# Packed attention and a feed-forward layer on one core: a new order table, aligned buffers at the end of SBUF, another ending of the last rows

## Chip, core and metric

The kernel runs on one core of one Trainium2 chip. The metric is the device time of the whole program in microseconds, as a median of runs. Engines are named as in the profile: PE (TensorE, with its weight loads as PEld), DVE (VectorE), ACT (ScalarE), POOL (GpSimd), SP (SyncE, which here only issues transfers).

## The reference

Eight batches of eight heads with 576 tokens of width 64 go through an attention over 32 learned packs: first the packs look at the tokens, then the tokens look at the packs. The result, 4608 tokens of width 512, goes through a feed-forward layer of width 2048.

```python
def sm_attn(qq, kk, vv):
    s = scale * np.matmul(qq, kk.transpose(0, 1, 3, 2))
    s = s - np.max(s, axis=-1, keepdims=True)
    a = np.exp(s)
    a = a / (np.sum(a, axis=-1, keepdims=True) + 1e-09)
    return np.matmul(a, vv)
p_packed = sm_attn(p, k, v)
attn = sm_attn(q, p_packed, p_packed)      # 8 x 8 x 576 x 64
x = attn.transpose(0, 2, 1, 3).reshape(4608, 512)
h = x @ w_in                               # 512 x 2048, float64
g = h * (1.0 / (1.0 + np.exp(-h)))
out = (g @ w_out).astype(np.float32)       # 2048 x 512, float64
```

## The kernel before

**Precision.** A float32 product is made from two parts of each factor, a rounded upper part and the rest (names end in hi and lo), and three products of those: hi·hi, hi·lo, lo·hi.

**Weights.** w_in and w_out arrive as the bits of float64 numbers and are turned into float32 on the chip, in 20 chunks. Each chunk n goes through the steps fetch (a transfer on SP's queue, L238), scale (two instructions on ACT, L244 and L245), clip (DVE, L249), sign (DVE, L253), shift (DVE, L261), join (POOL or DVE, L265); a chunk of w_out also through upper (ACT, L273) and lower (DVE, L277). Chunks 0 to 7 have 128 x 512 numbers, the others 128 x 1024.

**Attention of a batch.** For the packs: scores (L284), their largest values, exps on ACT (L331), a turn and a spread by 16 small transfers (L363), the packed product (L384), its scaling by the shares (L394, which writes the tile pp), and a turn back into ppT (L403, L407). For the tokens, in two halves: scores (L284), transposes on DVE (L420), largest values (L468), exps (L488), sums, shares, a turn, and the split into a_hi (L518, ACT) and a_lo (L522, DVE). Packed rows are multiplied by w_in ahead of time (L532, split at L550 and L553), so a batch's hidden values come from a product of its shares with pw_hi and pw_lo (L587).

**Feed-forward.** The work is cut into 144 units. A unit has a first product (L587), silu on ACT, the split of its values into g_hi and g_lo, and a product by w_out (L643) that adds into the four banks acc. Units 0 to 31 belong to batches 0 and 1 and run while the weights are still converted; they make g_hi on ACT (L599) and g_lo on DVE (L605). From unit 36 on, the units of batches 2 to 7 take two blocks of w_out at once in seven products in place of eight, for which some sums of values are made on POOL (L619 to L621), g_hi on ACT (L633) and g_lo on DVE (L637), and some sums of weights are kept in DRAM (sums_of_w). Those sums are formed once for each pair p of blocks, by DVE (L721), POOL (L726 to L729), ACT (L734) and DVE (L738). The 16 units of a batch are two passes of eight, one for each half of the tokens; each pass ends in pair_rows, which reads the four banks and stores 256 rows, and the next pass begins in the same banks. 32 rows of each half are left over; four of the units (32 to 35, 68 to 71, 104 to 107, 140 to 143) hold those of two batches each, and end in rest_rows (L767). The last of them ends the program.

**What sets the order.** Nothing here is found by a scheduler except for POOL's queue and the waits. A table of tokens, ORDER (lines 54 to 123), lists every step: a letter or two for the step, a number for the batch, unit or chunk. The instructions of PE, DVE, ACT and SP are issued in the order of that table. wf5 is the fetch of chunk 5, ws, wc, wz, wi, wj, wu and wl the further steps of a chunk; a small a with a letter is a step of attention (as scores of the packs, ax exps of the packs, aa packed product, aS, aT, aM the scores, transposes and largest values of the tokens); pf, pp, pu, pl belong to the packs' product by w_in; h, g, l, o are first product, silu with g_hi, g_lo and product by w_out of an early unit, and B, G, N, I, F, L, O the steps of a later one (B the first, O the last product); r, R, ru, rl, rk make the sums of weights of a pair; k, v and q load a batch; Wn runs n small matmuls; E is pair_rows, Y rest_rows.

**Buffers.** Pools named with side "right" are laid out from the far end of SBUF. First comes win there (the weights of w_in, int32), whose space goes to the pair buffers later: w_pair, w_sums, and the sums that come back from DRAM. The tile pp lies in the pool tmp on the other side.

## Time and profile before

| | us |
|---|---|
| median of three runs | 695.2 |
| lowest and highest run | 695.13, 695.38 |
| the profiled execution | 696.58 |
| its span | 694.80 |

The rows come from the profiled execution. A window is given in microseconds from the start of its span. The mean granted clock of TensorE over the span was 0.993 of full speed. An engine's busy time is the time in which an instruction of it ran; its idle time in brackets is put down to what came last.

### The profile page before, as it was taken

To read this page: it belongs to the slowest core of one execution; us is meant where nothing else is said; L and a number is where in the kernel's file an instruction comes from. 1 tells how busy PE (TensorE), PEld (TensorE's weight loads), DVE (VectorE), ACT (ScalarE), POOL (GpSimd) and SP (SyncE) were. 2 spreads that over 40 slices of the span, in tenths; PEclk is the share of its full clock that TensorE was granted. 3 is DMA by queue.
4 is the path that set the end of the run, shared out by engine and by line. 5 is a ranking of instruction groups with operands and counts; after the bars stand their busy time and mean duration, and the time that the engine had idled before them with its cause. 6 is when DMAs were issued, how large, how long until landed. Compare 5 with 4: busy or idle time off the path is not lost.

```text
span 694.8 us, 14721 instructions
## 1 busy us (share of the span) xinstructions
PE 674.6 (97%) x5958; PEld 593.1 (85%) x5958; DVE 425.9 (61%) x588; ACT 386.5 (56%) x641; POOL 232.4 (33%) x336
## 2 busy tenths in 40 slices
PE   7699999999999999999999999999999999999996
PEld 5477776788878998999888998899888998899995
DVE  5988989896774536753666525853665435663433
ACT  5787887453645535563555634755554753564431
POOL 0102054343203432544423333353241353435420
PEclk9899999999999999999999999999999999999999
DMA  9747864675967768867797578874984738685531
GB/s 362 321 138 300 289 218 174 232 267 193 367 242 290 267 223 328 360 253 260 284 339 284 186 276 328 336 268 130 364 346 174 290 120 324 252 317 184 218 132 45
DMA packets 55107, 178.62 MB, mean 257 GB/s; under 512 B 21760, under 2 KB 25856, under 8 KB 47360
## 3 DMA queue, kind: packets, MB, share of 16 engines
q1 hardware_dynamic: 54944, 177.56, 69.0%
q8 instruction: 47, 0.77, 0.4%
q10 hardware_dynamic: 96, 0.13, 0.1%
q14 instruction: 20, 0.16, 0.1%
HBM read 149.42 MB, written 24.12 MB: 250 GB/s over the span
## 4 chain that ended last, share of the span: by engine, by line
PE 77%; DVE 10%; ACT 4%; DMA 4%; SPq 2%; issue 2%; POOL 1%; ACTq 0%; DVEq 0%
PE ps_acc L643 46%; PE ps_two L587 24%; PE ps_two L284 5%; DMA win<-in_w_out 2%; PE ps_two L384 2%; DMA sums_of_w<-sums_of_w 2%; SPq L363 2%; DVE tm L420 1%; DVE g_lo L605 1%; DVE w_raw L249 1%; DVE w_raw L253 1%; DVE g_lo L637 1%; DVE wo_lo L277 1%; DVE o L785 1%; DVE win L261 0%
## 5 line engine op out<-in xcount | busy, mean ns | idle before, releaser
L637 DVE TENSOR_TENSOR g_lo<-g,g_hi 128x896 fp32r<-128x896 f32 x96 | 106.4, 1116 | 131.2 <-ACT g_hi L633 128.4
L643 PE MATMUL ps_acc<-wo_hi,g_hi 128*128 128x256 f32 (+1 forms) x576 | 185.1, 321 | 0.8 <-DVE o L785 0.8
L643 PE MATMUL ps_acc<-wo_hi,g_lo 128*128 128x256 f32 (+1 forms) x576 | 183.9, 319 | 2.0 <-DVE g_lo L605 2.0
L643 PE MATMUL ps_acc<-wo_lo,g_hi 128*128 128x256 f32 (+1 forms) x576 | 183.6, 319 | 0.0
L587 PE MATMUL ps_two<-a_hi,pw_hi 128*128 128x288 f32 x512 | 153.1, 299 | 1.5 <-DVE tm L420 1.5
L619 POOL TENSOR_TENSOR g<-g 128x128 f32<-128x128 f32 x96 | 56.4, 587 | 290.7 <-ACT g L609 290.6
L587 PE MATMUL ps_two<-a_lo,pw_hi 128*128 128x288 f32 x512 | 151.4, 296 | 0.0
L587 PE MATMUL ps_two<-a_hi,pw_lo 128*128 128x288 f32 x512 | 151.4, 296 | 0.0
L633 ACT CAST g_hi<-g 128x896 fp32r<-128x896 f32 x96 | 89.8, 940 | 76.7 <-POOL g L621 45.0
L643 PEld LDWEIGHTS ps_acc<-wo_hi,g_hi 128*128 128x128 f32 x576 | 108.4, 188 | 16.3 <-issue 5.6
L643 PEld LDWEIGHTS ps_acc<-wo_hi,g_lo 128*128 128x128 f32 x576 | 108.7, 189 | 12.4 <-DVE g_lo L605 4.3
L643 PE MATMUL ps_acc<-sums_of_w,g_hi 128*128 128x256 f32 x576 | 116.7, 284 | 0.3 <-DMA sums_of_w<-sums_of_w 0.3
L643 PEld LDWEIGHTS ps_acc<-wo_lo,g_hi 128*128 128x128 f32 x576 | 108.5, 188 | 7.1 <-DVE wo_lo L277 0.3
L587 PEld LDWEIGHTS ps_two<-a_hi,pw_hi 128*128 128x128 f32 x512 | 96.7, 189 | 14.4 <-PE ps_two L284 6.7
L587 PEld LDWEIGHTS ps_two<-a_lo,pw_hi 128*128 128x128 f32 x512 | 96.6, 189 | 0.8
L643 PEld LDWEIGHTS ps_acc<-sums_of_w,g_hi 128*128 128x128 f32 x576 | 89.1, 189 | 9.3 <-issue 7.8
L587 PEld LDWEIGHTS ps_two<-a_hi,pw_lo 128*128 128x128 f32 x512 | 96.6, 189 | 0.0
L643 PE MATMUL ps_acc<-sums_of_w,g_lo 128*128 128x256 f32 x288 | 81.2, 282 | 0.0
L620 POOL TENSOR_TENSOR g<-g 128x256 f32<-128x256 f32 x96 | 75.0, 783 | 6.6
L609 ACT ACTIVATE g<-ps_two 128x512 f32<-128x512 f32 x96 | 56.9, 597 | 33.4 <-DVE g_lo L637 16.9
L643 PEld LDWEIGHTS ps_acc<-sums_of_w,g_lo 128*128 128x128 f32 x288 | 54.6, 190 | 0.3 <-DVE g_lo L637 0.3
L621 POOL TENSOR_TENSOR g<-g 128x128 f32<-128x128 f32 x96 | 52.3, 546 | 6.6
(129 smaller groups left out, 798.9 us busy)
## 6 DMA issues: line engine op xcount, KB each, us to landing
sums_of_w<-sums_of_w SPq DMA_DIRECT2D x96, 768.0 KB, 6.3
w_quarter<-w_in SPq DMA_DIRECT2D x22, 1024.0 KB, 6.9
kvq_t<-in_v SPq DMA_DIRECT2D x8, 1280.0 KB, 8.8
kvq_t<-in_pkT SPq DMA_DIRECT2D x7, 1216.0 KB, 10.4
out<-o SPq DMA_DIRECT2D x16, 512.0 KB, 3.2
kvq_t<-in_qT SPq DMA_DIRECT2D x7, 1152.0 KB, 8.1
w_raw<-in_w_in SPq DMA_DIRECT2D x6, 1024.0 KB, 6.1
sums_of_w<-w_sums SPq DMA_DIRECT2D x8, 768.0 KB, 3.8
```

What stands on the lines that cost most here:

```text
L249: nc.vector.tensor_scalar(up.bitcast(F32), up.bitcast(F32), TOP, -TOP, op0=ALU.min, op1=ALU.max)
L284: nc.tensor.matmul(bank(par)[NP * i : NP * i + NP], lhs(r, i), rhs(r, i), start=True, stop=True)
L363: nc.sync.dma_start(self.e1T[NP * at : NP * at + NP, : some.shape[1], i], some)
L384: nc.tensor.matmul(self.ps[NP * i : NP * i + NP, par * D : par * D + D], e, vs[:n, c, h * D : h * D + D], start=(c == 0), stop=(c == 4),)
L587: nc.tensor.matmul(bank, p[:, par, cols], a[:, par], start=(n == 0), stop=(n == len(todo) - 1))
L609: nc.scalar.activation(g[:, : 4 * P].rearrange("p (e s) -> p e s", e=2), made["h", u, None][..., :MAIN], AF.Silu)
L619: nc.gpsimd.tensor_tensor(x[:, 4], x[:, 0], x[:, 2], ALU.subtract)
L620: nc.gpsimd.tensor_tensor(x[:, 5:7], x[:, 0:5:4], one, ALU.subtract)
L621: nc.gpsimd.tensor_tensor(x[:, 7], x[:, 3], x[:, 6], ALU.add)
L633: nc.scalar.copy(both[0], g)
L637: nc.vector.tensor_tensor(g_lo, g, g_hi.bitcast(F32), ALU.subtract)
L643: nc.tensor.matmul(out, g[:, rows], w, start=(first and n == 0), stop=(last and n == 2), skip_group_check=True)
```

## The change

Three things are edited: the order table, the place of some buffers, and the last rows. The instructions stay the same in number and kind, except that ACT loads function tables 46 times in place of 42 and that the last rows' store is one transfer in place of four.

**The table.** All of ORDER is replaced; the diff shows one line of each version, from the place where unit 59's product and unit 60's follow one another.

**Buffers.** A new pool, edge, is the first on the right side. It holds pp in 504 float32 numbers for each partition, 2016 bytes, of which 128 numbers are used. All other buffers of the right side move down by that much; they stood at 224 bytes beyond a multiple of 256 and now stand at multiples of 256.

**The last rows.** In the last four products of a rest unit, the blocks n = 0 and 2, which add into bank 0, come ahead of n = 1 and 3, which add into bank 2. In rest_rows the two additions change places: first the one between two parts of what ACT copied out of bank 0, then the one that reads bank 2. The four stores of 32 rows, on SP's queue and for the last batches also on ACT's, become one of 128 rows on SP's.

```diff
 ORDER = """
...
-O58 I59 F59 L59 G60 I60 F60 L60 O59 N61 G61 ar4 aa4 pf19 an4 S61 B62 E3.0 S62 S63 I61 ai4 aj4 O60 N62 F61 G62 L61
...
+B61 F59 N61 ai4 S59 S61 O58 S60 pf19 S62 L59 G61 I60 F60 B62 O59 N62 L60 E3.0 G62 O60 I61 F61 aj4 aS4.0 L61 I62 pp19
...
 """
 
 TP_BUFS = 4
+EDGE = 504
 ON_TOKENS = (0,)
...
     at_right = [ExitStack(), ExitStack()]
+    edge = ent(tc.tile_pool(name="edge", bufs=1, side="right"))
...
         def scaled1(self):
-            self.pp = tmp.tile([P, P], F32, name="pp", bufs=1)
+            self.pp = edge.tile([P, EDGE], F32, name="pp")[:, :P]
...
     def rest_products(u):
         b, f, _ = units[u]
         first, last = f == 0, f + FJ == NF
-        for n in range(FJ):
+        for n in sorted(range(FJ), key=lambda n: n % 2) if last else range(FJ):
...
         if opened.get(("rest", b, 0)):
             nc.scalar.copy(o[:, 1], acc[0])
+            nc.vector.tensor_tensor(o[:, 1, high], o[:, 1, high], o[:, 1, low], ALU.add)
             nc.vector.tensor_tensor(o[:, 0], acc[2], o[:, 1], ALU.add)
-            nc.vector.tensor_tensor(o[:, 0, high], o[:, 0, high], o[:, 1, low], ALU.add)
         else:
             nc.scalar.copy(o[:, 0, low], acc[2][:, low])
             nc.vector.tensor_copy(o[:, 0, high], acc[2][:, high])
-        for n, (e, h) in enumerate((e, h) for e in range(2) for h in range(2)):
-            at = (b + e) * S + h * HS + MAIN
-            rows = slice((2 * e + h) * REST, (2 * e + h) * REST + REST)
-            (nc.scalar if n % 2 and b == B - 2 else nc.sync).dma_start(out[at : at + REST], o[rows, 0])
+        to = out[b * S : (b + 2) * S].rearrange("(n s) e -> n s e", s=HS)[:, MAIN:]
+        nc.sync.dma_start(to, o[:, 0])
```

What the new table moves is seen best in the instructions of one engine. In the changed kernel a line's number is one or two higher than in the kernel before.

The first place is the start of SP's queue, which issues the loads. L238 (later L240) fetches a chunk of weights, L197 (L199) loads packs and keys of batch 0, L216 (L218) its values, L206 (L208) its tokens. Before:

```order
L238 DMA w_raw<-in_w_in 128x512
L197 DMA kvq_t<-in_pkT 128x1280
L197 DMA kvq_t<-in_pkT 128x1152
L238 DMA w_raw<-in_w_out 128x512
L216 DMA kvq_t<-in_v 128x2560
L238 DMA w_raw<-in_w_in 128x512
L206 DMA rest<-in_qT 128x1280
L206 DMA o<-in_qT 128x1024
L238 DMA win<-in_w_out 128x512
L238 DMA w_raw<-in_w_out 128x512
```

After:

```order
L240 DMA w_raw<-in_w_in 128x512
L240 DMA w_raw<-in_w_out 128x512
L199 DMA kvq_t<-in_pkT 128x1280
L199 DMA kvq_t<-in_pkT 128x1152
L240 DMA w_raw<-in_w_in 128x512
L240 DMA w_raw<-in_w_out 128x512
L240 DMA win<-in_w_out 128x512
L218 DMA kvq_t<-in_v 128x2560
L208 DMA rest<-in_qT 128x1280
L208 DMA o<-in_qT 128x1024
```

The second chunk moves ahead of the keys, and three chunks that stood behind the values and the tokens now stand ahead of the values.

The second place is DVE around the g_lo of unit 21. In the stretch before it is the first g_lo row (the second is unit 22's); w_raw is chunk 19 at L249, L253 and L261 (L251, L255 and L263), and the rows on w_pair are the pair sums of p = 4. Before, from the step behind the g_lo of unit 20:

```order
L407 COPY ppT<-ps_two 128x128
L738 TENSOR_TENSOR w_sums<-w_pair,w_sums 128x1024
L277 TENSOR_TENSOR wo_lo<-w_raw,wo_hi 128x1024
L605 TENSOR_TENSOR g_lo<-g,g_hi 128x512
L721 TENSOR_TENSOR w_pair<-wo_hi,wo_lo 128x2x256
L721 TENSOR_TENSOR w_pair<-wo_hi,wo_lo 128x512
L249 TENSOR_SCALAR w_raw<-w_raw 128x1024
L253 SCALAR_TENSOR_TENSOR w_raw<-w_raw 128x1024
L261 TENSOR_SCALAR w_raw<-w_raw 128x1024
L553 TENSOR_TENSOR pw_lo<-ps_two,pw_hi 128x1024
```

After, from the lower part of chunk 18 on; the first g_lo row is unit 20's, and unit 21's and 22's are the last row:

```order
L279 TENSOR_TENSOR wo_lo<-w_raw,wo_hi 128x1024
L607 TENSOR_TENSOR g_lo<-g,g_hi 128x512
L251 TENSOR_SCALAR w_raw<-w_raw 128x1024
L255 SCALAR_TENSOR_TENSOR w_raw<-w_raw 128x1024
L422 STREAM_TRANSPOSE tm<-ps_two 128x288 x2
L263 TENSOR_SCALAR w_raw<-w_raw 128x1024
L422 STREAM_TRANSPOSE tm<-ps_two 128x288 x2
L723 TENSOR_TENSOR w_pair<-wo_hi,wo_lo 128x2x256
L723 TENSOR_TENSOR w_pair<-wo_hi,wo_lo 128x512
L470 TENSOR_REDUCE mx_1673<-tm 128x18
L607 TENSOR_TENSOR g_lo<-g,g_hi 128x512 x2
```

Clip, sign and shift of chunk 19, the pair sums, two pairs of transposes and a maximum of batch 2 have moved from behind the g_lo of unit 21 to ahead of it.

The third place is ACT at the exps of batch 2's packs (tm and den), among the silu values g of the early units around number 10. Before:

```order
L598 ACTIVATE g<-ps_two 128x512
L599 ACTIVATE g_hi<-ps_two 128x512
L600 ACTIVATE rest<-ps_two 128x64
L550 CAST pw_hi<-ps_two 128x1024
L331 ACT_TABLE_LOAD
L331 ACTIVATE tm,den<-tm,nm 128x576 x2
L598 ACT_TABLE_LOAD
L598 ACTIVATE g<-ps_two 128x512
L599 ACTIVATE g_hi<-ps_two 128x512
L600 ACTIVATE rest<-ps_two 128x64
L734 CAST w_sums<-w_pair 128x1024
```

After:

```order
L600 ACTIVATE g<-ps_two 128x512
L601 ACTIVATE g_hi<-ps_two 128x512
L602 ACTIVATE rest<-ps_two 128x64
L333 ACT_TABLE_LOAD
L333 ACTIVATE tm,den<-tm,nm 128x576
L600 ACT_TABLE_LOAD
L600 ACTIVATE g<-ps_two 128x512
L601 ACTIVATE g_hi<-ps_two 128x512
L602 ACTIVATE rest<-ps_two 128x64
L333 ACT_TABLE_LOAD
L333 ACTIVATE tm,den<-tm,nm 128x576
L600 ACT_TABLE_LOAD
```

The two exps, which stood behind one table load, are now parted by the silu of a unit, so that four loads stand there in place of two.

## Rows read from the trace of the kernel before

**Rows 1.** The page: busy time, share and instructions of each engine, and the busy tenths of DVE in 40 slices of 17.4 us each.

```profile
PE 674.6 (97%) x5958; PEld 593.1 (85%) x5958; DVE 425.9 (61%) x588; ACT 386.5 (56%) x641; POOL 232.4 (33%) x336
...
DVE  5988989896774536753666525853665435663433
```

**Rows 2.** The table by stage, for the stretch in which weights are still converted and the one from there to unit 143. Columns: window, its length, then busy time and instructions of PE, of its weight loads, of DVE, ACT and POOL, granted clock, DMA share, GB/s.

```profile
26.60:125.70 99.10, 95.46 (x726) 74.57 (x727) 92.04 (x128) 77.25 (x128) 27.20 (x19) 0.97 0.60 215
125.70:675.70 550.00, 547.09 (x4911) 493.72 (x4910) 309.96 (x413) 290.04 (x479) 203.44 (x310) 1.00 0.72 266
```

**Rows 3.** The chain of waits between 120 and 156 us, in order of time: start, length, what ran. L605 makes the g_lo of an early unit, L643 is a product by w_out.

```profile
126.05 0.69 DVE g_lo L605
...
126.79 2.79 PE ps_acc L643 x10
...
151.87 3.00 PE ps_acc L643 x12
```

**Rows 4.** The transfers of all queues between 8 and 13 us, and the first instructions of the packed product of batch 0 in PE's timeline (start, length, engine, line, what; in brackets the idle time before and its releaser).

```profile
DMA packets 355, 2.09 MB, mean 418 GB/s; under 512 B 37, under 2 KB 37, under 8 KB 238
...
12.23 1.73 PE L384 MATMUL ps_acc<-kvq_t,tm 128*32 128x64 f32 x80 [0.46 <-DVE tm L370]
```

**Rows 5.** Groups of instructions of ACT from 0 to 31 us, by line and shape: busy time, mean ns of one, idle time before and its releaser; these are the scale steps of one chunk. Below them DVE's first instruction on a weight in its timeline.

```profile
L244 ACT ACTIVATE w_raw<-w_raw 128x512 int32<-128x512 uint32 x4 | 2.7, 687 | 2.6 <-DMA w_raw<-in_w_in 2.6
L244 ACT ACTIVATE win<-win 128x512 int32<-128x512 uint32 x4 | 2.6, 660 | 0.9 <-DMA win<-in_w_out 0.9
L245 ACT ACTIVATE w_raw<-w_raw 128x512 f32<-128x512 f32 x4 | 2.6, 659 | 0.0
...
5.80 0.43 DVE L249 TENSOR_SCALAR w_raw<-w_raw 128x512 f32<-128x512 f32 x1 [5.80 <-ACT w_raw L245]
```

**Rows 6.** The table by stage, columns as in rows 2: to the end of the second g_lo of unit 0, from that of unit 4 to that of unit 16, and from there to that of unit 21.

```profile
0.00:39.00 39.00, 29.91 (x345) 22.35 (x345) 28.78 (x59) 25.45 (x48) 4.19 (x9) 0.91 0.85 338
63.03:126.74 63.71, 61.37 (x398) 48.31 (x397) 60.07 (x75) 49.24 (x73) 21.43 (x15) 1.00 0.59 205
126.74:147.82 21.08, 21.03 (x193) 17.01 (x194) 16.94 (x22) 12.87 (x22) 5.17 (x5) 1.00 0.73 267
```

**Rows 7.** DVE's timeline: the clip of chunk 13, clip and sign of chunk 17, then the pair sums of p = 4, clip and sign of chunk 19, and two transposes of batch 2.

```profile
86.57 0.69 DVE L249 TENSOR_SCALAR w_raw<-w_raw 128x1024 f32<-128x1024 f32 x1
...
111.38 2.38 DVE L249 TENSOR_SCALAR w_raw<-w_raw 128x1024 f32<-128x1024 f32 x1
113.80 1.23 DVE L253 SCALAR_TENSOR_TENSOR w_raw<-w_raw 128x1024 int32<-128x1024 int32 x1
...
147.74 1.28 DVE L721 TENSOR_TENSOR w_pair<-wo_hi,wo_lo 128x512 f32<-128x512 f32 x2
149.29 1.17 DVE L249 TENSOR_SCALAR w_raw<-w_raw 128x1024 f32<-128x1024 f32 x1 [0.27 <-ACT w_raw L245]
150.50 1.63 DVE L253 SCALAR_TENSOR_TENSOR w_raw<-w_raw 128x1024 int32<-128x1024 int32 x1
...
154.33 0.83 DVE L420 STREAM_TRANSPOSE tm<-ps_two 128x288 f32<-128x288 f32 x2
```

**Rows 8.** POOL's timeline around 151 us: the third of the four pair sums of p = 4.

```profile
151.13 1.60 POOL L728 TENSOR_TENSOR w_pair<-w_pair 128x256 f32<-128x256 f32 x1
```

**Rows 9.** Waits of PE from 199.5 to 675.7 us, by the line that waited and what released it: us in total, times, longest.

```profile
PE ps_two L587 <- DVE tm L420: 1.2, 5, 0.2
PE ps_two L284 <- DVE tm L420: 0.5, 2, 0.2
```

**Rows 10.** PE's timeline: two matmuls of unit 99, and the first of unit 140.

```profile
507.98 0.28 PE L643 MATMUL ps_acc<-sums_of_w,g_hi 128*128 128x256 f32 x1
508.31 0.39 PE L643 MATMUL ps_acc<-sums_of_w,g_lo 128*128 128x256 f32 x1
...
679.12 0.47 PE L643 MATMUL ps_acc<-wo_hi,g_hi 128*128 128x512 f32 x1 [0.75 <-DVE o L785]
```

**Rows 11.** The end of the program: ACT, DVE and the queues in the timeline, then the transfers from 690 us on and, for its size, one of 512 KB between 676 and 685 us (queue, number, KB each, median us from issue to landing).

```profile
689.66 0.59 ACT L769 COPY o<-ps_acc 128x512 f32<-128x512 f32 x1 [4.36 <-PE ps_acc L643]
...
690.40 0.69 DVE L770 TENSOR_TENSOR o<-ps_acc,o 128x512 f32<-128x512 f32 x1 [4.38 <-PE ps_acc L643]
691.12 0.42 DVE L771 TENSOR_TENSOR o<-o 128x256 f32<-128x256 f32 x1
691.57 0.80 SPq L778 DMA_DIRECT2D out<-o  x2
...
out<-o SPq DMA_DIRECT2D x2, 64.0 KB, 1.7
out<-o ACTq DMA_DIRECT2D x2, 64.0 KB, 1.9
...
out<-o SPq DMA_DIRECT2D x1, 512.0 KB, 2.7
```

**Rows 12.** Waits of DVE from 31 to 126 us, columns as in rows 9.

```profile
DVE w_sums L738 <- ACT w_sums L734: 1.7, 1, 1.7
...
DVE pp L394 <- PE ps_two L384: 0.7, 1, 0.7
```

**Rows 13.** ACT's timeline: the load of a function table, and the exps behind it.

```profile
97.66 1.28 ACT L331 ACT_TABLE_LOAD   x1
98.95 0.78 ACT L331 ACTIVATE tm<-tm,nm 128x576 f32<-128x576 f32 x1
```

More of the change, by code (lines that the diff above doesn't have):

```diff
@@ L121 @@
+O132 N134 L133 N135 G134 G135 I134 O133 S135 F134 I135 B137 L134 F135 L135 B136 N136 G136 O134 N137 I136 G137 O135
+I137 F136 L136 B138 G138 I138 F137 L137 O136 S138 F138 L138 B139 S137 O137 S139 O138 G139 N138 I139 F139 L139 F140
+L140 O139 E7.1 N139 O140 F141 L141 F142 O141 F143 L142 L143 O142 O143 Y6
 """
 TP_BUFS = 4
+EDGE = 504
 ON_TOKENS = (0,)
```

123 lines of the change are left out of this document (60 added, 63 removed).

## The prediction

> **What bounds the kernel now.** I read the page first: TensorE (PE) is busy for 97% of the span, but VectorE (DVE) has its dense slices only in the first fifth [rows 1]. So the limit changes on the way, and an average over the span says nothing. The table by stage shows where: from 26.6 to 125.7 us DVE is busy for 92 of 99 us, from there to 675.7 us PE for 547 of 550 [rows 2]. The chain of waits puts the joint at one place: it comes over DVE as far as the g_lo of unit 16, which starts at 126.05, and from 126.79 us it stays on PE's products [rows 3]. So two sums matter: how much PE work is still ahead when PE stops waiting for DVE, and what PE loses after that. A third is the tail behind PE's last product, which ends at 690.3 [rows 11].
>
> The sum is made against the profiled execution: 696.58 us, 1.78 of them outside its span of 694.80. It lies 1.38 us above the median of 695.2; I work out the difference and take it from the median.
>
> **The new order, first 150 us.** I added up what stands on DVE ahead of an instruction in each version, every step with its duration in the trace.
>
> *The start.* The loads form one queue, which moved 418 GB/s from 8 to 13 us [rows 4]. It is in order, so v of batch 0 now has three more chunks of 512 KB ahead: 1.57 MB at 418 GB/s, 3.8 us. ScalarE (ACT) has three more scale steps ahead of the copy that the packed product needs, each two instructions of 0.69 and 0.66 us [rows 5], 3.7 us with their overlap, and what they scale lands first. The packed product began at 12.23 us [rows 4] and now begins near 16.0. The attention of batch 0 is then 3.8 us late, but DVE does weight steps meanwhile: 4.1 us more of them stand ahead. By the second g_lo of unit 0, which ended at 39.0 us, this is level: 29.0 us of DVE work ahead, against 28.8 [rows 6]; ahead of unit 4's, 50.5 against 50.7. So I cost the new start at nothing; its cover is that DVE has chunks to convert while the attention waits. Without it the price is at most what DVE has idled to that point once data was there, 39.0 - 28.8 = 10.2 us less the 5.8 before its first step [rows 5], 4.4 us.
>
> *Unit 16.* The clip and the sign of chunk 17 (2.38 and 1.23 us [rows 7]) go behind its g_lo. With unit 4's 0.2 us and smaller moves DVE has 107.4 us ahead of it instead of 110.7, and PE could leave the stretch that DVE sets 3.3 us sooner.
>
> *Unit 21 takes that back.* Ahead of its g_lo stand now clip, sign and shift of chunk 19 (the first two 1.17 and 1.63 us), the pair sums of p = 4 (1.28), and two pairs of transposes (one pair 0.83) and a maximum of batch 2 [rows 7]: 7.4 us more, 135.1 instead of 127.7. From the g_lo of unit 4, at 62.8 us, that leaves 60.07 + 16.94 + 7.4 + 0.2 = 84.6 us of DVE work. Idle time: between units 4 and 16 DVE was idle for 63.71 - 60.07 = 3.6 us [rows 6]; at that pace 84.6 us of work bring 5.1. The g_lo ends at 62.8 + 84.6 + 5.1 = 152.5 us, and the product of unit 21 starts at 152.6. Before, it started at 151.87 [rows 3]; PE now has one scores step of 0.5 us more ahead of it, so 152.4 would be level: +0.2. But the clip of 1.17 and the sign of 1.63 us ran beside POOL's pair sums (one of them 1.60 us [rows 8]); the like clip alone took 0.69 and the like sign 1.23 [rows 7]. Now these steps stand ahead of the pair sums and so escape them: 0.9 us less. POOL then runs beside other DVE steps, so I take half, and get **-0.3 us**. Bounds: after unit 16 DVE idled for 21.08 - 16.94 = 4.1 us because PE led [rows 6]. If nothing of that is left and the 0.9 us is gained in full, the g_lo ends at 147.82 + 7.4 - 4.1 - 0.9 = 150.2, which gives -2.1. If all of it is left, 155.2, and +2.9.
>
> **The new order, 200 to 676 us.** Here PE sets the time, so an order pays only where PE waited.
>
> - Packs products behind a scores product: PE waited there for DVE's transposes 5 + 2 times, 1.7 us in all [rows 9], 0.24 each. The new order keeps 2 of the 7 places: **-1.2 us**; bounds 0 (the wait moves on) and -1.7.
> - Units 59 and 60 are the end and the start of two passes over the same four sums. A first product and the packed product of batch 4 stood between them and hid the read-out of the sums by ACT and DVE; now nothing does. The like case before, between units 139 and 140, waited 0.75 us [rows 10]. Unit 60 begins in the bank that is read first, though: **+0.5**; bounds 0.2 and 0.8.
> - Between the two products of a unit its values pass ACT, POOL, ACT and DVE. The tightest distance before, the last unit's aside, is 5.7 us of PE work (units 39, 80, 93, 99). Unit 99 stood still there, its third matmul at 508.31, 0.2 us late behind that of 507.98 [rows 10]. Now unit 111 has 5.1 us and 78, 110, 113, 114 have 5.7. I take 0.3 for two of them: **+0.6**; bounds 0 and 2.
>
> Together -0.1, bounds -1.5 and +2.8. Two of the four added table switches fall into this part, 2.6 us of an ACT that is busy for 290 of 550 us [rows 2], which hides them.
>
> **The shift by 32 bytes.** The same scale instruction took 660 ns on win, which was not on such a multiple, and 687 on w_raw, which was [rows 5]. Nothing to win: **0**, bounds -0.3 and 0.
>
> **The last rows.** The last chain is PE, L770 at 690.40, L771 at 691.12 for 0.42 us, the transfers at 691.57 [rows 11]. L771's work now comes first: the even products come ahead, so their bank is complete three matmuls (0.7 us) sooner, the copy of 0.59 us that began at 689.66 begins at 689.0, and the addition of 0.42 us behind it is over at 690.0. That is before PE's end; its cover is a DVE that stood idle for 4.38 us there [rows 11]. It saves 691.57 - 691.12, some 0.44 us. Of two transfers on each queue the later was issued at about 692.0 and landed 1.9 us later, 693.9. One of 256 KB, issued at 691.13, lies between 1.7 us for 64 KB and 2.7 for 512 KB [rows 11]; on a straight line 2.1, so it lands at 693.2: **-0.7 us**; bounds -1.1 (with 1.7) and -0.1 (with 2.7). The Trainium skill (DMA: Bandwidth & Descriptors, Anatomy of one DMA) gives a transfer 2.0 us and its bytes at 436 GB/s, an estimate of 2.6 us here and a gain of 0.2; the row of 64 KB, 1.7 us, is already below the fixed part.
>
> **Sum:** -0.3 - 0.1 + 0 - 0.7 = -1.1 us, so 694.1.
>
> **Rivals.**
> *The early order pays in full.* DVE's longest wait between units 4 and 16, 1.7 us for ACT's w_sums [rows 12], is gone, since POOL forms those sums 40 us sooner. If nothing takes its place, unit 21 gives -2.1; with -0.7 in the main part, where units 60 and 111 then cost half, and -0.7 in the tail: -3.5, 691.7 us. For it: that wait is nearly half of the 3.6 us. Against it: the packed product of batch 2 now comes ahead of unit 16, and that of batch 1 cost DVE 0.7 us [rows 12].
> *Table switches on the path.* Around units 10 and 11 ACT goes exp, silu, exp, silu now: four loads of 1.28 us [rows 13] where two stood, 2.6 us ahead of the values of these units. If DVE has nothing else then, they become idle time: the g_lo of unit 21 ends at 152.5 + 2.6 = 155.1, +2.8, with -0.1 and -0.7 +2.0, 697.2 us. It decides from 3 us of idle time beside those 5.1. For it: the longest of DVE's waits there is already one for ACT [rows 12]. Against it: 5 us of weight steps and pair sums stand on DVE between those units' values. The Trainium skill (ScalarE: Activation LUTs, What ACT_TABLE_LOAD costs) adds a drain of 1.38 us to each switch; that would be 5.3 us, and 699.9. Here the load ends at 97.66 + 1.28 = 98.94 and the next instruction starts at 98.95 [rows 13], so I keep 1.28.
> *The order does nothing,* and only the tail counts: 694.5. This is within the forecast's own case.
>
> **How the numbers follow.** Within 0.2% (693.8 to 696.6, about what a measurement here can tell from no change): 0.40, and the likeliest; alone it would have 693.2 to 695.6. The first rival: 0.38. Slower, by the second or by more at units 111 to 114: 0.22. The range reaches to 690.9, the first rival with 0.8 of the main part's lower bound, and to 697.9, the second with 0.7 of its upper one.
>
> **What would show it.** Right: unit 16's g_lo some 3 us sooner; unit 21's product near 152 us, with a wait for g_lo; two waits of PE behind scores products instead of seven; half a microsecond at unit 60; 3.8 us from PE's end to the end of the span instead of 4.5. Wrong: unit 21 not waiting, DVE idle for over 8 us between units 4 and 21, or late loads of sums_of_w in the main part. These I left out, since each stands on SP behind the same kind of work as before.

## The result

| | us | against before |
|---|---|---|
| before, median of 4 runs | 695.29 (695.13 to 695.96) | |
| changed kernel, median of 4 runs | 703.87 (702.75 to 704.57) | 1.012 times, 95% interval 1.0102 to 1.0138 |
| its profiled execution, span | 704.49, 702.7 | |

It is slower by 8.6 us, where the forecast had 694.1 and a range up to 697.9. In the two spans, 694.8 and 702.7, PE's last matmul ends at 690.3 and 695.1: 4.8 us are lost before that end and 3.1 behind it.

**The tail.** First ACT's copy, the two additions and the store in the timeline of the changed kernel, to be set beside [rows 11].

```profile
693.75 0.59 ACT L771 COPY o<-ps_acc 128x512 f32<-128x512 f32 x1 [3.68 <-PE ps_acc L645]
...
694.38 0.43 DVE L772 TENSOR_TENSOR o<-o 128x256 f32<-128x256 f32 x1 [3.58 <-ACT o L771]
...
695.12 0.69 DVE L773 TENSOR_TENSOR o<-ps_acc,o 128x512 f32<-128x512 f32 x1 [0.31 <-PE ps_acc L645]
695.83 0.61 SPq L778 DMA_DIRECT2D out<-o  x1
```

The exchange worked: L772 is over before PE ends, and the store goes out 0.75 us behind PE's end, where it took 1.27. But the span ends 6.9 us behind that store. The transfers from 694 us on in the changed kernel (DMA: busy share of the 16 engines in tenths, in 40 slices), then those of the last transfers in the kernel before, from 690 us on:

```profile
DMA  0000000000000024112301312222222210000000
...
DMA packets 132, 0.26 MB, mean 30 GB/s; under 512 B 4, under 2 KB 4, under 8 KB 132
```

```profile
DMA  0000000000000000000079679899610000000000
...
DMA packets 192, 0.26 MB, mean 55 GB/s; under 512 B 64, under 2 KB 64, under 8 KB 192
```

The same bytes; but the DMA engines are busy by one to four tenths, for over four microseconds, where they were by six to nine tenths, and only 4 packets are under 512 B where four transfers had 64. These small ones close a transfer, one for each DMA engine that took part: 4 engines here, 16 for each of the old stores. Each of the 4 had 32 rows of 2 KB in line; 4 busy of 16 are 2.5 tenths.

**Up to unit 21.** The table by stage of the changed kernel, columns as in rows 2: to the second g_lo of unit 0, from that of unit 4 to that of unit 16, and from there to that of unit 21.

```profile
0.00:40.23 40.23, 30.97 (x339) 23.09 (x340) 30.69 (x61) 25.18 (x46) 8.28 (x14) 0.92 0.84 330
...
63.01:126.04 63.03, 62.31 (x493) 50.16 (x492) 59.60 (x74) 46.74 (x71) 14.63 (x11) 1.00 0.57 204
126.04:153.50 27.46, 26.04 (x186) 20.10 (x185) 26.56 (x32) 16.22 (x25) 9.78 (x8) 1.00 0.85 316
```

Against [rows 6] DVE's idle time between units 4 and 21 fell, from 3.64 + 4.14 to 3.43 + 0.90 us. Its busy time rose from 60.07 + 16.94 to 59.60 + 26.56 us, by 9.2, where the forecast had 7.6 less half of 0.9. The g_lo of unit 21 ended at 153.5, and PE's product (the last line here is PE's timeline, the others DVE's and POOL's) began at 153.13, not at 152.1.

```profile
113.24 2.98 DVE L723 TENSOR_TENSOR w_pair<-wo_hi,wo_lo 128x512 f32<-128x512 f32 x2
...
149.62 2.45 DVE L723 TENSOR_TENSOR w_pair<-wo_hi,wo_lo 128x512 f32<-128x512 f32 x2
...
152.66 0.84 DVE L607 TENSOR_TENSOR g_lo<-g,g_hi 128x512 fp32r<-128x512 f32 x1
```

```profile
113.40 2.27 POOL L267 TENSOR_TENSOR w_raw<-w_raw 128x1024 int32<-128x1024 int32 x1 [4.11 <-DVE w_raw L263]
```

```profile
153.13 0.50 PE L645 MATMUL ps_acc<-wo_hi,g_hi 128*128 128x512 f32 x1
```

The pair sums of p = 4, 1.28 us for two instructions in [rows 7], took 2.45, and those of p = 2 took 2.98: one instruction of POOL, the join of chunk 15, stood beside them from 113.40 to 115.67.

But PE didn't wait for that g_lo. PE's waits from 100 to 155 us, in the changed kernel and then before:

```profile
PE ps_two L286 <- DVE win L267: 1.4, 1, 1.4
PE ps_acc L645 <- DVE g_lo L607: 0.2, 1, 0.2
```

```profile
PE ps_acc L643 <- DVE g_lo L605: 2.0, 3, 1.3
```

The wait of 1.4 us is that of one packs' product by w_in (the step pp8) for the join of chunk 17. PE's line of it, then DVE's clip and join of that chunk:

```profile
136.23 1.09 PE L286 MATMUL ps_two<-win,ppT 64*32 64x512 f32 x16 [1.42 <-DVE win L267]
```

```profile
130.35 1.24 DVE L251 TENSOR_SCALAR w_raw<-w_raw 128x1024 f32<-128x1024 f32 x1
...
134.44 1.64 DVE L267 CUSTOM_DVE_ANT_0 win<-w_raw,win 128x2048 uint16<-128x2048 uint16 x1
```

The new table has the clip and the sign of chunk 17 behind the values of units 16 and 17. DVE does its four steps without a pause, from 130.35 to 136.08, and POOL's four additions for p = 3 stand beside them from 129.98 to 135.0. The like steps took 0.68, 1.23, 0.70 and 1.23 us with no addition beside them, 1.9 us less in all than here.

**The main part.** PE's waits from 199.5 to 680 us, as in [rows 9].

```profile
PE ps_two L589 <- ACT rest L615: 0.8, 2, 0.5
PE ps_acc L645 <- DVE o L773: 0.8, 1, 0.8
PE ps_two L286 <- DVE tm L422: 0.2, 1, 0.2
PE ps_two L589 <- DVE tm L422: 0.2, 1, 0.2
```

Two waits for transposes are left of seven, as forecast. New are waits for ACT's values (L615) and for rest_rows (L773).

To follow PE through runs whose order differs, I use its **loss**: the time that its steps took beyond the shortest time of a step of the same kind in the kernel before, added up. At 50, 150, 200 and 690 us it was 17.9, 24.4, 25.4 and 37.9 us before.

### The profile page after: what moved, and what is told of

It is laid out like the page before. It is cut to its first block, busy times and chain, and to the rows that moved or that the text cites. A ratio compares the mean times of both kernels' runs of the same rounds, so it can differ in the third digit from the quotient of the medians.

```text
span 702.7 us, 14710 instructions
## 1 busy us (share of the span) xinstructions
PE 679.2 (97%) x5958; PEld 597.0 (85%) x5958; DVE 433.3 (62%) x588; ACT 391.8 (56%) x645; POOL 230.7 (33%) x336
## 5 line engine op out<-in xcount | busy, mean ns | idle before, releaser
L639 DVE TENSOR_TENSOR g_lo<-g,g_hi 128x896 fp32r<-128x896 f32 x96 | 110.0, 1148 | 141.2 <-ACT g_hi L635 140.9
L621 POOL TENSOR_TENSOR g<-g 128x128 f32<-128x128 f32 x96 | 52.5, 547 | 291.8 <-ACT g L611 272.9
L635 ACT CAST g_hi<-g 128x896 fp32r<-128x896 f32 x96 | 89.9, 940 | 74.5 <-POOL g L623 49.1
L645 PE MATMUL ps_acc<-sums_of_w,g_hi 128*128 128x256 f32 x576 | 118.3, 287 | 0.1
L622 POOL TENSOR_TENSOR g<-g 128x256 f32<-128x256 f32 x96 | 73.4, 765 | 6.9
L623 POOL TENSOR_TENSOR g<-g 128x128 f32<-128x128 f32 x96 | 59.2, 617 | 6.9
L615 ACT ACTIVATE rest<-ps_two 128x64 f32<-128x64 f32 x96 | 20.7, 223 | 63.6 <-PE ps_two L589 63.3
```

The lines of the kernel that those rows point to most:

```text
L615: nc.scalar.activation(rest[:, 2 * p : 2 * p + 2, b % 2, hf], made["h", u, None][..., MAIN:HS], AF.Silu)
L621: nc.gpsimd.tensor_tensor(x[:, 4], x[:, 0], x[:, 2], ALU.subtract)
L622: nc.gpsimd.tensor_tensor(x[:, 5:7], x[:, 0:5:4], one, ALU.subtract)
L623: nc.gpsimd.tensor_tensor(x[:, 7], x[:, 3], x[:, 6], ALU.add)
L635: nc.scalar.copy(both[0], g)
L639: nc.vector.tensor_tensor(g_lo, g, g_hi.bitcast(F32), ALU.subtract)
```

## The experiments

Each time is a median beside runs of the kernel before in the same session (695.6 to 696.0); the changed kernel's own stood at 695.29. So a difference between runs of two sessions is uncertain by some 0.4 us.

### The parts alone

**tail_only** is the kernel before with the edits of rest_products and rest_rows, **shift_only** with EDGE, the pool edge and pp's place, **order_only** with the new table. **four_stores** is the changed kernel with the old stores:

```diff
-        to = out[b * S : (b + 2) * S].rearrange("(n s) e -> n s e", s=HS)[:, MAIN:]
-        nc.sync.dma_start(to, o[:, 0])
+        for n, (e, h) in enumerate((e, h) for e in range(2) for h in range(2)):
+            at = (b + e) * S + h * HS + MAIN
+            rows = slice((2 * e + h) * REST, (2 * e + h) * REST + REST)
+            (nc.scalar if n % 2 and b == B - 2 else nc.sync).dma_start(out[at : at + REST], o[rows, 0])
```

> The kernel before with the edits of the last rows alone: even blocks first, the two additions exchanged, one transfer of 128 rows. In the changed kernel the last transfer was issued at 695.84 and landed near 701.6, 5.8 us later, with the DMA engines 0.1 to 0.3 busy. Theory A (the one transfer is served by few of the 16 DMA engines, whatever the order table is): the end comes 5.8 us after the issue in place of 1.9, less some 0.4 us for the earlier issue and 0.4 for the single issue: +3.1 us against before, about 698.4. Rival (the transfer is late because something else of the new program holds the queue): no more than 0.3 us from before, and rather 0.7 below it, as forecast.

699.08 us, 1.0045 times before (1.0033 to 1.0058): +3.0. Theory A holds.

> The kernel before with the buffers of the right side moved to multiples of 256 bytes and nothing else. In the changed kernel the median product of a pair unit took 2.514 us of PE in place of 2.495, and that of an early unit 2.743 in place of 2.804. Theory B (the place of the buffers sets this): 96 x 0.02 = +1.9 us, less up to 16 x 0.06 = 1.0 us for the early units from unit 16 on, where PE sets the time: +1 to +2 us. Rival (the new order does it, by what runs beside the products): 0 within 0.3 us, and both medians as before.

697.26 us, 1.0019 (1.0010 to 1.0028): +1.2. The median product of a pair unit, from its first matmul to the start of what follows, went from 2.495 to 2.514 us, that of an early unit from 2.804 to 2.741. Theory B holds.

> The kernel before with the new order table and nothing else. Theory B: the stalls of the new order remain, units 63, 65, 72, 110 and 114 among them, and unit 21 one us late: +2 to +4 us, with 2.495 us for the median product of a pair unit. Rival (the order does all that is not the tail): +4.8 us, with 2.514. The forecast had -0.4 for it.

697.95 us, 1.0037 (1.0024 to 1.0051): +1.9, with 2.495 for a pair unit. In its profile PE ends 2.8 us later than before; the loss at 50, 150 and 200 us is 19.5, 25.4 and 26.2, and from 200 us on it grows by 14.6, where before had 12.5.

> The changed kernel with the four stores of 32 rows in the old form on both queues; the exchanged additions stay. Theory A: the last store lands 1.9 us after its issue as before, 3.5 us sooner than the one transfer less 0.4 for the second issue on the queue: about 700.3 us in place of 703.9, with DMA engines 0.6 to 0.9 busy in the last 2 us. Rival: the time stays at 703.9 within 0.5.

700.82 us, 1.0069 (1.0056 to 1.0081): 3.1 us less than the changed kernel. The last 256 KB left 64 packets under 512 B again.

### The one transfer

**two_stores** cuts it in two, of which ACT issues the second:

```diff
-        nc.sync.dma_start(to, o[:, 0])
+        for n in range(0, 4, 2):
+            (nc.scalar if n and b == B - 2 else nc.sync).dma_start(to[n : n + 2], o[n * REST : n * REST + 2 * REST, 0])
```

> The changed kernel with the last rows stored by two transfers of 2 x 32 rows, one on SP's queue and one on ACT's, in place of one of 4 x 32. In the profile the one transfer of 4 pieces left 4 packets under 512 B, each of the old ones of 32 rows 16. Theory A (each outermost piece of a transfer goes to one DMA engine, so 32 packets of 2 KB stand in line on each of 4): two transfers of two pieces still use 4 engines with 32 packets each, and the end stays at 703.9 within 0.4, with 4 packets under 512 B in all. Rival (a transfer's time goes by its bytes): half the bytes on each of two queues, 2 us sooner, about 701.9.

709.38 us, 1.0186 (1.0164 to 1.0209): 5.5 us slower still than the changed kernel, or 4.9 with each beside its own runs of before. Both theories had missed that. The transfers from 693 us on:

```profile
DMA packets 132, 0.26 MB, mean 16 GB/s; under 512 B 4, under 2 KB 4, under 8 KB 132
...
q1 hardware_dynamic: 66, 0.13, 3.3%
q10 hardware_dynamic: 66, 0.13, 2.3%
```

Each transfer left 66 packets, 64 rows and 2 small ones: two DMA engines each. The last row started 7.3 us behind the first, where in the one transfer it was 4.1, so both transfers stood on the same two engines; in the trace two packets are in flight at a time, in the one transfer four, in the old stores 14 to 16. (The profiled span is 5.3 us longer: PE ends 2.3 us later, with the granted clock at half once more, from 237.7 to 241.1 us, and the transfers make the other 3.0.) The Trainium skill says both things (DMA: Bandwidth & Descriptors, Why a DMA increments its semaphore by 16 and not by 1): a transfer from SP or ACT uses the largest number of engines up to 16 that divides the outermost dimension of both sides, and takes the lowest-numbered ones. For 4 x 32 rows that is 4 and for 2 x 32 it is 2, and the packets agree.

### The place of the buffers

**pad_below** and **sums_128** are the kernel before with unused buffers on the right side; pad_below has the second line alone, with 56 numbers in place of 32:

```diff
+    ent(tc.tile_pool(name="edge", bufs=1, side="right")).tile([P, 24], F32, name="edge")
...
+    pad = at_right[1].enter_context(tc.tile_pool(name="pad", bufs=1, side="right")).tile([P, 32], F32, name="pad")
     gp = at_right[1].enter_context(tc.tile_pool(name="gp", bufs=2, side="right"))
```

> The kernel before with an unused buffer of 224 bytes between the pair buffers and the early units' values: g, g_hi and g_lo of the early units move to multiples of 256 bytes, sums_of_w stays at 224 beyond one. Theory B with its two halves apart: the median early product falls from 2.80 to 2.74 us, which from unit 16 on is worth up to 1.0 us, and the product of a pair unit stays at 2.495: -1.0 us against before, between -0.6 and -1.3. Rival (both depend on the same buffers): pair units go to 2.514 as well, and the time is +1.

695.00 us, 0.9984 (0.9976 to 0.9993): -0.95, with 2.742 for an early product and 2.495 for a pair unit's. The two halves are separate. Groups of PE's instructions by line and shape (count, busy time, mean ns of one), before, shift_only and pad_below in turn; a busy time of PE is modelled, but the direction is that of the starts:

```profile
L643 PE MATMUL ps_acc<-sums_of_w,g_lo 128*128 128x256 f32 x288 | 81.2, 282 | 0.0
...
L643 PE MATMUL ps_acc<-wo_lo,g_hi 128*128 128x512 f32 x192 | 75.7, 394 | 0.0
```
```profile
L645 PE MATMUL ps_acc<-sums_of_w,g_lo 128*128 128x256 f32 x288 | 81.7, 284 | 0.0
...
L645 PE MATMUL ps_acc<-wo_lo,g_hi 128*128 128x512 f32 x192 | 75.3, 392 | 0.0
```
```profile
L644 PE MATMUL ps_acc<-sums_of_w,g_lo 128*128 128x256 f32 x288 | 81.2, 282 | 0.1
...
L644 PE MATMUL ps_acc<-wo_lo,g_hi 128*128 128x512 f32 x192 | 75.2, 392 | 0.0
```

In shift_only, with sums_of_w at a multiple of 256, its matmuls last 284 ns in place of 282; with the early values there, wo_lo by g_hi goes from 394 to 392. But in the same view the matmuls of 128x256 with wo_hi and wo_lo, which did not move, went from 281 to 283 ns as well. So the 0.019 us of a pair unit come from the place of the pair buffers; that it is the reading of sums_of_w alone isn't shown.

> The kernel before with early values at multiples of 256 bytes as in pad_below, but the pair buffers and sums_of_w at 128 bytes beyond one, in place of 224. With 0 (shift_only) the product of a pair unit took 2.514 us, with 224 2.495. If only a place off the multiples of 256 counts, 2.495 and pad_below's time, 695.0; if the multiples of 64 or 128 count, 2.514 and about 697.0.

695.40 us, 0.9996 (0.9987 to 1.0005), and 2.498 for a pair unit, near the 2.495 of a place 224 beyond a multiple of 256. The time is 0.4 to 0.8 above pad_below's, of which 96 x 0.003 = 0.3 would come from that. Three places were tried, 0, 128 and 224, and only 0 cost much.

### The start and the granted clock

**order_warm** and **order_warm9** are order_only with small matmuls on PE in the idle time ahead of aU0.0, **before_warm** is the kernel before with the like at its own place.

```diff
-aE0.0 aU0.0 aE0.1
+aE0.0 W20 aU0.0 aE0.1
```

> The kernel before with the new order alone and 20 more small matmuls on PE ahead of the first unpacking product of batch 0 (2.2 us at full clock), where PE stood idle from 28.5 to 30.8 us. In the profiles of the changed kernel and of order_only the granted clock was at half from 31 to 38 us, right behind that idle stretch, and PE had lost 19.45 us at 50 us; in act_order, whose order is the same up to there, the half clock came at 19.8 to 23.2 us and the loss was 17.5. Theory E (the half clock behind that idle stretch is what the new start costs): full clock from 31 to 38 us, a loss near 17.5 at 50 us, and some 2 us less than order_only, 696.0 where order_only had 697.95. Rival (DVE sets the time there whatever PE's clock): the clock is full and the time as order_only's within 0.4.

699.27 us, 1.0053 (1.0040 to 1.0065), 1.3 above order_only. The clock was full from 14.4 us on, but the 20 matmuls were more than the idle time held.

> The kernel before with 22 more small matmuls at the same step, where PE stood idle from 22.4 to 25.1 us; the half clock lay from 26.7 to 33.5 us. Theory E: the stretch at half clock goes or moves, and as PE has 4.7 us of work less in it than the new order has, the gain is smaller: 0.5 to 1.5 us. Rival: DVE sets the time from 26.6 us on, and nothing changes within 0.4.

696.57 us, 1.0012 (1.0003 to 1.0020): 0.6 slower, with the clock full from 18.5 us on. On the kernel before the rival holds.

> order_warm with 9 small matmuls in place of 20. In order_warm the clock was full from 14.4 us on, but the 20 took 4.6 us (0.23 each, not the 0.11 that I had put down), from 28.3 to 32.9, so they held up the work that was ready at 30.8. Nine take 2.1 us and end near 30.5. Theory E: full clock from 31 to 38 us, the product of unit 4 near 63.0 us as in act_order (65.0 in order_only), and 2 us less than order_only's profiled execution: 697.0 or less. Rival (the clock there doesn't matter): as order_only, 697.9.

697.52 us, 1.0031 (1.0020 to 1.0041). The table by stage from 28 to 40 us, columns as in rows 2, of the changed kernel and then of order_warm9:

```profile
28.00:32.00 4.00, 1.68 (x10) 0.94 (x8) 3.86 (x10) 4.00 (x7) 0.00 (x0) 0.87 1.01 428
32.00:36.00 4.00, 4.00 (x34) 2.31 (x41) 3.31 (x7) 1.81 (x4) 1.42 (x1) 0.50 0.64 268
36.00:40.00 4.00, 3.96 (x34) 2.99 (x19) 3.09 (x7) 3.52 (x9) 0.00 (x0) 0.77 0.50 161
```
```profile
28.00:32.00 4.00, 3.68 (x30) 3.07 (x29) 3.86 (x10) 4.00 (x7) 0.00 (x0) 1.00 1.00 425
32.00:36.00 4.00, 3.50 (x46) 2.13 (x46) 4.00 (x9) 3.64 (x5) 1.42 (x1) 1.00 0.73 281
36.00:40.00 4.00, 3.84 (x23) 3.42 (x24) 4.00 (x8) 3.52 (x14) 0.00 (x0) 1.00 0.81 320
```

In the changed kernel PE is busy for 1.68 of four microseconds, and the clock behind that is 0.50, 1.2 GHz, while the attention and first units of batch 0 stand on PE; DVE then waits, busy for 6.40 of 8 us where it is 8.00 of 8 at full clock. With the idle time filled, unit 4's product starts at 63.13 in place of 65.03 us, and the profiled execution takes 697.39 us in place of order_only's 699.36. So theory E holds for such an execution. The median gains nothing that is clear of the noise: +1.9 against its own session's before, as order_only. Of order_only's five times three are 697.6 to 698.0 already and two 699.4 and 699.9, of which 699.36 alone is profiled; that the half clock is missing from the faster ones is argued, not shown. It does differ between executions: in the profiles of act_order, late_steps and order_mended, whose order is the same up to there but for order_mended's small matmuls, it lay around 20 to 24 us and not behind 31.

### Around unit 21

**late_19** and **late_steps** are order_only with chunk 19 moved back behind unit 21's g_lo; the second:

```diff
-g20 l20 ws19 wc19 b0 o19 aS2.0 aS2.1 wz19 aT2.0 o20 wi19 aT2.1 r4 aM2.1 h21 g21 l21 wj19
+g20 l20 ws19 b0 o19 aS2.0 aS2.1 aT2.0 o20 aT2.1 h21 g21 l21 wc19 wz19 wi19 r4 aM2.1 wj19
```

> The kernel before with the new order alone, but scores, clip, sign, shift, transposes, the pair sums of p = 4 and the maximum moved back behind the g_lo of unit 21 (7 us of DVE work). In order_only PE had lost 1.0 us more than before at 150 us and 0.7 more at 200. Theory C (these steps make unit 21 late, and that is the early part's whole loss): no wait for unit 21, and 0.7 to 1.0 us less than order_only's 697.95. Rival: the same work makes one of units 22 to 31 late, and the loss at 200 us is as in order_only.

704.00 us, 1.0113 (1.0099 to 1.0127), 6.0 above order_only. I had moved two scores products along with the steps, and the first product of unit 22 stood behind them.

> The kernel before with the new order alone; clip, sign and shift of chunk 19, the pair sums of p = 4 and a maximum stand behind the g_lo of unit 21 again, while scores and transposes stay, so that no product stands in line behind them (in late_19 the first product of unit 22 did: PE stood still from 151.9 to 154.5 us, and its clock fell). From 125 to 150 us PE lost 2.2 us in order_only and act_order and 1.3 in before. Theory C: unit 21 no longer waits, and the loss of this stretch is 1.3 or less: 1 us below order_only, given that the clock is the same. Rival: the steps moved back make units 22 to 25 late, and the loss at 200 us less that at 125 stays at 3.0.

703.53 us, 1.0113 (1.0099 to 1.0127), 5.6 above order_only. Unit 21's product starts at 151.30, but that is no gain: with the steps still ahead of it it starts at 151.35 in act_order and at 151.24 in order_warm9, and order_only's 153.41 comes from the half clock at the start. So theory C had the wrong place: it was the packs' product that waited, and it still does, 1.2 us. The loss from 125 to 200 us is 8.9 us. The rival holds. PE's timeline, then ACT's, then a line of the table by stage:

```profile
157.85 0.61 PE L587 MATMUL ps_two<-a_hi,pw_hi 128*128 128x288 f32 x1 [3.49 <-ACT rest L600]
```

```profile
155.58 1.12 ACT L273 CAST wo_hi<-w_raw 128x1024 fp32r<-128x1024 f32 x1 [5.59 <-POOL w_raw L265]
156.61 0.59 ACT L598 ACTIVATE g<-ps_two 128x512 f32<-128x512 f32 x1
```

```profile
158.00:162.00 4.00, 4.00 (x17) 4.00 (x18) 4.00 (x5) 2.61 (x4) 1.73 (x2) 0.50 0.00 0
```

ACT's upper part of chunk 19 (L273) waits for POOL's join and stands ahead of the silu of unit 22 in ACT's queue; PE waits 3.5 us for that, and its clock is at half from 156.9 to 163.7 us. Bringing chunk 19 forward, as the new table does, has a reason; in the two ways tried it couldn't be undone alone.

**order_short_sums** is order_only with three of POOL's four additions for each pair left out and the fourth cut to 8 columns.

> The kernel before with the new order alone; of POOL's four additions for each pair of blocks of w_out three are left out and the fourth is cut to 8 columns, so the sums of weights are not formed. In the trace of order_only six instructions of DVE ahead of the g_lo of unit 21 ran beside those additions and took 2.6 us more than the same instructions alone. Theory G (POOL's work stretches DVE's, and the forecast priced DVE by durations that had another neighbour): these six take 0.68 and 1.22 us, and PE loses 1 to 2 us less between 75 and 150 us than the 3.3 of order_only. Rival (DVE's time there is set by its own work): the same durations, and 3.3 us.

696.23 us, 1.7 below order_only, 1.5 with each beside its own before; 1.0007 times before (0.9997 to 1.0016). Its profiled execution took 1304 us, with PE's steps at about twice their time, so neither PE's loss nor the wait of the packs' product can be read from it; in that profile, with no additions beside them, the six instructions of DVE take 0.68 to 0.69 and 1.22 to 1.23 us. The time speaks for theory G, in particular for the wait of the packs' product, but which wait went isn't shown.

### The main part

**act_order** is order_only with

```diff
-L62 aX4.0 aD4.0 O62 B64 G64 aM4.1 N64 F63 L63 B65
+L62 aX4.0 F63 aD4.0 L63 O62 B64 G64 aM4.1 N64 B65
...
-ax7.0 B110
+ax7.0 ax7.1 B110
...
-O111 ax7.1 ar7
+O111 ar7
```

> The kernel before with the new order alone and two edits in the main part: unit 63's g_hi and g_lo ahead of the silu of unit 64 instead of behind it, and the second exps of batch 7's packs beside the first instead of five units later. In order_only unit 66's first product waited for ACT and unit 63's product came late, 0.70 and 0.36 us, and unit 115's first product 0.43. Theory D (a table load of ACT, 1.28 us, stands ahead of the values that PE waits for, in ACT's queue): 0.36 of unit 63 and 0.43 of unit 115 go, 0.7 may stay, since the silu of unit 64 still follows a load: -0.8 us against order_only, 697.2. Rival (ACT is late there by its sum of work): both waits stay within 0.1 us.

697.29 us, 1.0021 (1.0011 to 1.0031): 0.7 below order_only, 0.6 with each beside its own before. The losses of units 63 and 115 are gone, that ahead of unit 66 fell from 0.70 to 0.18; unit 110's product lost 1.10 in place of 0.52, since both exps now stand ahead of its values. What the queue looked like in the changed kernel, ACT's timeline and one line of PE's:

```profile
341.92 1.28 ACT L490 ACT_TABLE_LOAD   x1
...
345.33 1.28 ACT L611 ACT_TABLE_LOAD   x1 [1.43 <-issue]
346.62 0.60 ACT L611 ACTIVATE g<-ps_two 128x512 f32<-128x512 f32 x1
347.12 0.22 ACT L615 ACTIVATE rest<-ps_two 128x64 f32<-128x64 f32 x1
347.22 0.94 ACT L635 CAST g_hi<-g 128x896 fp32r<-128x896 f32 x1
```

```profile
347.39 0.40 PE L589 MATMUL ps_two<-a_hi,pw_hi 128*128 128x288 f32 x1 [0.53 <-ACT rest L615]
```

The exp of batch 4's tokens (L490) brings a load, then the silu of unit 64 another at 345.33, which waits for PE; the g_hi of unit 63 (L635), whose input POOL had ready at 343.8, comes behind both.

**swap_at_end** is four_stores with the exchange only for the last two batches:

```diff
+            if b == B - 2:
+                nc.vector.tensor_tensor(o[:, 1, high], o[:, 1, high], o[:, 1, low], ALU.add)
             nc.vector.tensor_tensor(o[:, 0], acc[2], o[:, 1], ALU.add)
+            if b < B - 2:
+                nc.vector.tensor_tensor(o[:, 0, high], o[:, 0, high], o[:, 1, low], ALU.add)
```

> The four_stores kernel with the two additions of rest_rows exchanged for the last batches only. In it, unit 72's product lost 1.03 us behind rest_rows, in order_only, with the old additions, 0.34. Theory F (the exchanged addition stands ahead of the read of bank 2 on DVE, and unit 72 waits for that bank): the loss at unit 72 falls to 0.34, and the time to 700.1 from 700.8. Rival: the loss is from L73, which stands ahead of both, and stays at 1.0.

698.96 us, 1.0049 (1.0035 to 1.0063), 1.9 below four_stores. In the profiles the loss at unit 72 fell from 1.03 to 0.32; the rest of the difference lies ahead of that unit. Theory F holds. DVE's timeline in the changed kernel, and PE's behind it:

```profile
384.49 1.45 DVE L639 TENSOR_TENSOR g_lo<-g,g_hi 128x896 fp32r<-128x896 f32 x1 [1.76 <-ACT g_hi L635]
385.86 0.68 DVE L772 TENSOR_TENSOR o<-o 128x256 f32<-128x256 f32 x1
386.57 0.69 DVE L773 TENSOR_TENSOR o<-ps_acc,o 128x512 f32<-128x512 f32 x1
```

```profile
387.31 0.39 PE L645 MATMUL ps_acc<-wo_hi,g_hi 128*128 128x256 f32 x1 [0.77 <-DVE o L773]
```

**order_mended** joins order_warm9, act_order, swap_at_end's additions, pad_below's buffer and one more edit, B62 moved from ahead of O59 to behind it.

> The new order with all that the runs point to: nine more small matmuls ahead of the first unpacking product, the two edits of act_order, the first product of unit 62 between the products of units 59 and 60, the exchanged additions for the last batches alone with the four stores, and 224 unused bytes as in pad_below. Units 59 and 60 had lost 0.30 and 0.34 us in order_only; the forecast put 0.5 on that. If the steps add up: order_only's 697.95 - 0.4 (small matmuls) - 0.7 (act_order) - 0.5 (units 59 and 60) - 1.4 (pad_swap) = 694.9, and under 0.2 us lost at unit 60. Rival: the freed time is lost at the next unit, 695.5 or more.

696.61 us, 1.0015 (1.0006 to 1.0024). The rival holds. The first product of unit 62 did not hide the read-out. ACT's and PE's timeline:

```profile
328.81 0.22 ACT L614 ACTIVATE rest<-ps_two 128x64 f32<-128x64 f32 x1 [3.20 <-PE ps_two L588]
328.93 0.37 ACT L790 COPY o<-ps_acc 128x256 f32<-128x256 f32 x1
```

```profile
330.08 0.50 PE L644 MATMUL ps_acc<-sums_of_w,g_hi 128*128 128x256 f32 x2 [1.30 <-DVE o L789]
```

ACT's copy for pair_rows (L790) now stands behind a value of unit 62 (L614), which waits for that very product; unit 60 begins at 330.08, 1.3 us behind it.

**pad_swap** is the kernel before, old order and old stores, with pad_below's buffer, even blocks first and swap_at_end's additions; **pad_swap_warm** has W10 ahead of aU0.0 as well.

> The kernel before, its order and its four stores, with the unused 224 bytes of pad_below and with the exchanged additions for the last batches alone, even blocks first. By the parts measured apart: -0.95 for the buffers, -0.45 for the exchanged addition: 1.4 us below before, 694.5. If the parts don't add up, between 694.5 and 695.5.

694.33 us, 0.9982 (0.9973 to 0.9990): 1.25 us faster than before, the two parts added up (1.4 expected). It beats both kernels.

> pad_swap with 10 more small matmuls (2.3 us) ahead of the first unpacking product of batch 0, where PE stands idle from 22.4 to 25.1 us; in before_warm 22 of them took 5.1 us and held up that product by 1.9 us. Theory E: the half clock of before, 26.7 to 33.5 us, moves or goes, and 0.5 to 1.0 us is won on top of pad_swap. Rival (DVE sets the time there): as pad_swap within 0.3.

694.24 us, 0.9982 (0.9973 to 0.9991): the small matmuls add nothing.

## Why the prediction was wrong, step by step

**The last rows: -0.7 forecast, +3.0 measured, the largest miss.** The exchanged addition gave what was forecast, 0.5 us. The step that failed is "One of 256 KB ... lies between 1.7 us for 64 KB and 2.7 for 512 KB; on a straight line 2.1". I priced a transfer by its bytes; it went by the number of DMA engines that it is spread over, and took 5.8: the rows alone stood in line for 4.1 us, where before they took 1.1. No row of before shows a transfer on 4 engines, so an upper bound of 2.7 was a guess at size where the shape was new. The packets under 512 B would have told that 16 engines took part in each of the old ones, and the page of the Trainium skill that I cited for its fixed time has the rule for the shape. (The 2.0 us cited there are that page's fit for transfers that GpSimd issues; SP and ACT issued these.)

**The exchange in the middle of the program** was costed only at the end. At unit 72 PE waits for bank 2, and there the exchanged addition is in front of that bank's read: +0.7, with the new order only; tail_only has no loss there.

**The shift: 0 forecast, +1.2 measured.** I judged it by two instructions of ACT, and the bounds -0.3 and 0 by those alone. The sign differs by buffer: -0.95 for the early values alone, and in sum +1.2 for the whole shift, which makes each of 96 pair units 0.019 us longer.

**The start: 0 forecast.** The packed product came at 15.63 (16.0 forecast). But "its cover is that DVE has chunks to convert while the attention waits" left out PE's clock: the new order has its idle stretch right ahead of the attention of batch 0. In the profiles whose clock is at half behind that stretch, unit 4's product starts some 2 us later, at 65.03; in act_order's, whose half clock came earlier and was shorter (19.8 to 23.2 us), at 63.02, against 62.74 before.

**Units 16 and 21: -0.3 forecast.** In the changed kernel's profile unit 16's g_lo came 0.7 us sooner, not 3.3, but behind the half clock of the start; in act_order's, whose order is the same up to there, 2.6 sooner (123.46 in place of 126.05), and unit 21's product 0.45 sooner (151.35 in place of 151.80). So at full clock the number was about right, but by luck: PE never waited for unit 21's g_lo, and "Unit 21 takes that back" is the step that failed. The "unit 21 not waiting" of the signs of being wrong came true. I had summed DVE's work ahead of two g_lo's alone and left out another thing that PE takes from DVE: the packs' product needs the join of chunk 17, whose clip and sign I had moved back, and there 1.4 us were given back. "The like clip alone took 0.69 ... 0.9 us less" named POOL's effect and had its sign wrong: the same instructions of DVE took 5.2 us more in all up to unit 21, since other ones came to stand beside POOL's joins and additions, chunk 17's steps among them. The clip and sign that I had named, chunk 19's, did take 0.69 and 1.23. The Trainium skill (SBUF — State Buffer, Who interferes with whom) has DVE and GpSimd share a pair of ports that one of them holds for a whole instruction; a join of 2.27 us with an instruction of 2.38 in place of 0.68 beside it agrees.

**The main part: -0.1 forecast, +2.1 measured** (order_only's loss from 200 us on). Right were the waits behind scores products (steps on packs took 1.4 us less, 1.2 forecast), units 59 and 60 (0.64 us lost where before had 0.28; +0.5 forecast) and one of the tight distances (unit 110, 0.52). The step that failed is "an ACT that is busy for 290 of 550 us, which hides them": a table load costs nothing by ACT's average, and a wait where values for PE stand behind it. Units 63, 66 and 115 lost 1.5 us, and act_order won back 0.6 to 0.7 of the time. The rival on table switches had the mechanism and the wrong place, units 10 and 11.

**Sum.** order_only, shift_only and tail_only give 1.9 + 1.2 + 3.0 = 6.1, and unit 72 another 0.7; 1.8 of the 8.6 us are not assigned by the medians. In the two profiled executions, whose spans differ by 7.9 us, the account closes: 3.1 us are lost behind PE's end and 4.8 ahead of it, these all from 200 us on: 2.1 as in order_only, 1.9 as in shift_only and 0.7 at unit 72. So the 1.8 are most likely the spread of executions, which four runs don't settle: the new order's differ by 2 us, and the median of before beside the changed kernel lies 0.3 to 0.75 us below those of the later sessions. Of the main part's 2.1 us 1.3 stay in act_order (a loss of 13.8 from 200 us on, against 12.5 before); units 110, 60 and 72 hold some 1.8 there, and two waits of 0.4 that before had are gone, so the rest is small waits that no run took apart.

## What to carry to other kernels

Before stores are merged into one transfer, look at its outermost dimension on the DRAM side: four rows of blocks are four DMA engines, and the count of packets under 512 B tells how many took part. A reordering is not priced by the durations of its instructions alone: what stands beside them on POOL, and what stands behind a table load or a wait in ACT's queue, moves with it. Every product that takes something from the moved instructions has to be followed, not only the values that were the limit before. An edit in a function that is called several times has to be costed at each call, and a gain at the end of a program may be a loss in the middle.

## What the runs showed of the hardware

- Two transfers of 2 x 32 rows of 2 KB, issued by SP and by ACT, ran on the same two DMA engines: issuing from two queues won nothing and cost 3 us against one transfer on four.
- With the pair buffers and sums_of_w at a multiple of 256 bytes, PE's 21 matmuls of a pair unit took 2.514 us, at 128 or 224 beyond one 2.498 and 2.495. With the loaded values of the early units (g_hi, g_lo) it was the other way: their 12 matmuls took 2.80 us at 224 beyond one, 2.74 at a multiple.
- After PE had stood idle from 28.5 to 30.8 us, the granted clock was at 1.2 GHz from 31.0 to 37.8 us in the changed kernel and from 31.5 to 38.3 in order_only; in late_steps it was from 156.9 to 163.7, around the end of 3.5 us of idle time. In act_order, with the same order up to there, it stayed full behind an idle stretch from 28.9 to 30.7 us, but was at 1.2 GHz from 19.8 to 23.2. So the same order can have it at another place in another execution.
